# The second layer of a routed MLP with two blocks of 128 tokens per pass on the partitions, and w2 in row quarters

## Chip, core and metric

The kernel runs on one core of a Trainium2 chip. The metric is the device time of one execution in microseconds, the median of several runs. TensorE is called PE, VectorE DVE, ScalarE ACT, GpSimd POOL; SyncE (SP) only issues transfers here. Everything is fp32 unless said otherwise.

## What is computed

An RWKV-5 attention block is followed by a mixture-of-experts layer with one expert per token. The reference, cut:

```python
# attention: batch 4, 8 heads, 768 steps, head size 48
for t in range(S):
    cur = einsum('bhd,bhe->bhde', u * k_t, v_t)
    y[:, :, t] = einsum('bhd,bhde->bhe', r_t, state + cur)
    state = w * state + einsum('bhd,bhe->bhde', k_t, v_t)
# routing: N = 3072 tokens, 384 wide, 8 experts, hidden size 1024
logits = x @ w_gate
expert_idx = argmax(logits, axis=1)
gate_w = softmax(logits)[arange(N), expert_idx]
for e in range(E):
    mask = expert_idx == e
    h = maximum(x[mask] @ w1[e], 0)
    out[mask] = gate_w[mask] * (h @ w2[e])
```

## The kernel before

`straight` (line 42) does all the work, with the order of instructions on each engine written out by hand; `general` (line 672) is run instead only when a flag says that the data do not fit (an expert with more than 416 tokens, for one).

**Attention.** A loop of 16 steps (line 535), one for each batch and pair of heads, works in chunks of 128 time steps. In step i PE computes the own-token terms (`p_own`, line 263), the scores (275), the chunk states (298), the outputs of step i-1 (318, 323) and the transposition of step i-2 (`p_tr`, 336) so that tokens stand on partitions. ACT writes the diagonals (281) and copies the transposed outputs of step i-2 into the token buffer `xbs` of its batch (`keep`, 341 and 342; two buffers, so batch b+2 writes over batch b). POOL copies one element of `own` (542, so that it starts after DVE has read it), multiplies r and k for the next step (`pairs`, 250), and in most steps scales its keys (`keys`, 254). When the four steps of a batch are through, DVE picks each token's expert and a rank within the expert. POOL then sends each column of 128 tokens to the scratch tensor `rows` in HBM (`send`, 388), one row per token in the order of expert and rank, with the gate value and the token's number beside the token. The dictionary `sends` (503) says in which step of the loop which of the six columns of a batch go. In step 13 SP issues the loads of the early passes from `rows`; those of `rows` are ordered behind all sends put down before them.

**Experts.** Each expert has room for 416 tokens. For experts 0 and 1 the first 160 tokens are an early pass each, started while the last batch is still being routed; the late passes are the remaining 256 tokens of experts 0 and 1, and 416 tokens of each of experts 2 to 7. A pass does this:
- `load` (418): four transfers bring the tokens from `rows` into `xs`, 32 tokens by 32 columns at a time; there are three such buffers.
- `xT` (425): three DVE transposes of 32x32 blocks give the tokens with the features on the partitions.
- `L1` (430): for each of 8 hidden tiles of 128, three matmuls (line 435) with w1 as the stationary operand and all tokens of the pass moving; ACT applies the ReLU (437).
- `L2` (439): for each of 3 output tiles m, 8 matmuls (446) with a 128x128 block of w2 stationary and the tokens moving. A DVE transpose (448) turns the result back into 32x32 blocks. The three results stand in the PSUM banks `yps[0]`, `dsb`, `yps[1]` (`ybank`, line 68).
- `put` (477): DVE computes the destination of each piece and multiplies by the gate (488), and POOL scatters one group of 32 tokens after the other (491). A group is 128 pieces of 96 columns, so 416 tokens take 13 scatters.

Only the last pass (expert 7) has something else: its `L2` covers the first 160 tokens (`LAST`), and `tokens_out` (454) does the other 256 as two blocks of 128 tokens. There the tokens of the hidden layer are the stationary operand and w2 moves (467), in three pieces of 128 columns for each block; the token is then on the partition, the gate is a scalar per partition (470), and one scatter writes 128 whole rows (471). Gate and number for these come by a small load of their own (`load_ids`, 452). The two blocks use the banks `yps[0]` and `dsb`.

Each fp32 matmul of the program is two instructions in the profile; a hidden tile's w2 product of 416 tokens is thus two rows.

w1 of an expert is loaded in four quarters, w2 in three thirds, one for each m (`weights2`, 407); both have two buffers. All loads stand in one queue on SP, in the order of the program. The main loop (643) does for pass k: L1 of pass k; the transposes of pass k+1; w1 of expert e+2; then L2 and put of pass k-1 and the w2 of its expert plus 2; then the load of pass k+2. For the last pass L2 of pass 6 comes first, then L1 of pass 7, then the put of pass 6, L2 of pass 7 and `tokens_out`.

Of the kernel before, what the change touches and what calls it, by code (L numbers as in the profile page):

```python
# [17 lines left out]
B, H, S, D = 4, 8, 768, 48  # L18
E, F = 8, 1024
DM = H * D  # L20
N = B * S
HP = H // 2
# [19 lines left out]
def straight(tc, rk, vk, w, w1, w2, out, flag):  # L42
# [20 lines left out]
    dsb = pp.tile([128, 512], FP32, name="dsb")  # L63
    tr = pp.tile([128, 512], FP32, name="tr")
# [3 lines left out]
    ybank = [yps[:, 0, :], dsb, yps[:, 1, :]]  # L68
# [95 lines left out]
    pos2 = cp.tile([128, 4], FP32, name="pos2")  # L164
    it = cp.tile([128, 64], I32, name="it")
# [39 lines left out]


    w1s = [[cp.tile([128, DT, FQ], FP32, name=f"w1s{i}{q}") for q in range(4)] for i in range(2)]
    w2s = [[cp.tile([128, FT, 128], FP32, name=f"w2s{i}{m}") for m in range(DT)] for i in range(2)]
    ge = EARLY // 32

    def buffers(pool, n, k, x=None):
# [5 lines left out]
    early_bufs = [buffers(cp, EARLY, f"e{k}") for k in range(2)]  # L217
    cnt = cp.tile([128, E], FP32, name="cnt")
# [185 lines left out]
        for q in range(4):  # L404
            nc.sync.dma_start(w1s[e % 2][q], w1[e % E, q])

    def weights2(e, ms=range(DT)):
        for m in ms:
            nc.sync.dma_start(w2s[e % 2][m], w2[e % E, m])

    class Pass:
        def __init__(self, e, s0, n, bufs=None):
            self.e, self.s0, self.n = e, s0, n
            self.g = n // 32
            if bufs:
                self.x, self.t, self.h, self.y, self.yo, self.ix = bufs

        def load(self):
            for a in range(4):
                nc.sync.dma_start(  # L420
                    self.x[32 * a:32 * a + 32, 0:self.g, :],
                    rows[self.e * N + self.s0:self.e * N + self.s0 + self.n, a * Q:(a + 1) * Q].rearrange(
                        "(g j) c -> j g c", j=32))

        def xT(self):
            for m in range(DT):
# [9 lines left out]
                                     rhs=self.t[:, m, 0:self.n], start=m == 0, stop=m == DT - 1, skip_group_check=True)  # L436
                nc.scalar.activation(h[:, f, 0:self.n], p[:, 0:self.n], func=ACT.Relu)  # L437

        def L2(self, ms=range(DT), n=None):
            n = n or self.n  # L440
            g = n // 32
            y = self.y
            for m in ms:
                p = ybank[m]
                for f in range(FT):
                    nc.tensor.matmul(p[:, 0:n], lhsT=w2s[self.e % 2][m][:, f, :],  # L446
                                     rhs=self.h[:, f, 0:n], start=f == 0, stop=f == FT - 1, skip_group_check=True)
                nc.vector.transpose(y[:, 0:g, 32 * m:32 * m + 32], p[:, 0:n].rearrange("p (g j) -> p g j", j=32))  # L448

        def load_ids(self):  # L450

            nc.sync.dma_start(xg, rows[self.e * N + LAST:self.e * N + CAP, 2 * D:2 * D + 2].rearrange("(t p) c -> p t c", p=128))

        def tokens_out(self):

            nc.vector.tensor_scalar(out=vt, in0=pos2[:, 0:nl], scalar1=float(LAST), scalar2=cnt[:, self.e:self.e + 1],
                                    op0=ALU.add, op1=ALU.is_lt)
            nc.vector.memset(it2, 1 << 20)
            nc.vector.tensor_scalar(out=ia, in0=xg[:, :, 1].bitcast(I32), scalar1=2, scalar2=None,
                                    op0=ALU.logical_shift_right)  # L460
            nc.vector.copy_predicated(it2, vt, ia)
            for t in range(nl):
                p, y = ybank[t], yt[t].rearrange("p (a m i) -> p m a i", a=HP, m=DT)
                for m in range(DT):
                    o = p[:, m * 128:(m + 1) * 128]
                    for f in range(FT):
                        nc.tensor.matmul(o, lhsT=self.h[:, f, LAST + t * 128:LAST + (t + 1) * 128],  # L467
                                         rhs=w2s[self.e % 2][m][:, f, :], start=f == 0, stop=f == FT - 1,
                                         skip_group_check=True)
                nc.vector.tensor_scalar_mul(y, p[:, 0:DM].rearrange("p (m a i) -> p m a i", a=HP, m=DT), xg[:, t, 0:1])  # L470
                s_ = nc.gpsimd.indirect_dma_start(
                    out=out[:, :], out_offset=bass.IndirectOffsetOnAxis(ap=it2[:, t:t + 1], axis=0),
                    in_=yt[t][:, :], in_offset=None, bounds_check=N - 1, oob_is_err=False)
                tc.declare_no_dep(s_.ins, group="sc", reason="each token stands in one row")
                tc.add_to_no_dep_group("sc", s_.ins)

        def put(self, n=None):

            yo, ix, g = self.yo, self.ix, (n or self.n) // 32
            ids = self.x[:, 0:g, 2 * D + 1].bitcast(I32)  # L480
            if self.s0 == 0 and self.n == EARLY:
                nc.vector.tensor_copy(ix[:, 0:g], ids)
            else:
                nc.vector.tensor_scalar(out=vm[:, 0:g], in0=pos[:, 0:g], scalar1=float(self.s0), scalar2=cnt[:, self.e:self.e + 1],
                                        op0=ALU.add, op1=ALU.is_lt)
                nc.vector.memset(ix[:, 0:g], 1 << 20)
                nc.vector.copy_predicated(ix[:, 0:g], vm[:, 0:g], ids)
            nc.vector.tensor_tensor(yo[:, 0:g, :], self.y[:, 0:g, :], bc(self.x[:, 0:g, 2 * D:2 * D + 1], [128, g, 2 * D]),  # L488
                                    op=ALU.mult)
            for k in range(g):  # L490
                s_ = nc.gpsimd.indirect_dma_start(  # L491
                    out=out4[:, :], out_offset=bass.IndirectOffsetOnAxis(ap=ix[:, k:k + 1], axis=0),
                    in_=yo[:, k, :], in_offset=None, bounds_check=N * HP - 1, oob_is_err=False)
                tc.declare_no_dep(s_.ins, group="sc", reason="each token stands in one row")
                tc.add_to_no_dep_group("sc", s_.ins)

    LAST = 160
    early = [Pass(e, 0, EARLY, early_bufs[e]) for e in range(2)]
    late = [Pass(e, EARLY, CAP - EARLY) for e in range(2)] + [Pass(e, 0, CAP) for e in range(2, E)]

    sends = {}
    for b in range(B - 1):
        for k, cs in enumerate(((0,), (1, 2), (3, 4, 5)) if b < B - 2 else ((0,), (1, 2, 3, 4, 5))):
            sends[4 * b + 6 + k] = (b, cs)

    selection()
# [26 lines left out]
    for i in range(1, U):  # L535
        b, k = divmod(i - 6, 4)
# [78 lines left out]
    mp = P.enter_context(tc.tile_pool(name="mp", bufs=1))  # L615
    bufs = [buffers(mp, CAP, k) for k in range(2)]
    xss = [bufs[0][0], bufs[1][0], mp.tile([128, ng, Q], FP32, name="xs2")]
    for k, p in enumerate(late):
        _, p.t, p.h, p.y, p.yo, p.ix = bufs[k % 2]
        p.x = xss[k % 3]  # L620
    vm = mp.tile([128, ng], I32, name="vm")
    nl = (CAP - LAST) // 128
    xg = mp.tile([128, nl, 2], FP32, name="xg")
    vt, it2, ia = [mp.tile([128, nl], I32, name=n) for n in ("vt", "it2", "ia")]
    yt = [mp.tile([128, DM], FP32, name=f"yt{k}") for k in range(nl)]

    in_range()
    count(cnt)
# [7 lines left out]
    late[-1].load_ids()  # L636
    for p in early:
        p.L2()
        p.put()
# [24 lines left out]


# [6 lines left out]
def general(tc, rk, vk, w, w1, w2, out):  # L672
# [270 lines left out]
                half(b, hp, hf, kT, rT, vt, St, xb)  # L943
        gate(b, xb)
    for e in range(E):
        for m in range(DT):
            nc.scalar.dma_start(w2_all[:, e, :].rearrange("p (f m j) -> p m f j", m=DT, j=128)[:, m], w2[e, m])
    att.close()


# [181 lines left out]
def _layout(inputs):  # L1132
# [23 lines left out]
    w2 = x["moe_w2"].reshape(E, FT, 128, HP, DT, 32).transpose(0, 2, 1, 4, 3, 5).reshape(E, 128, FT, DT, 128)  # L1156
    w2 = w2.transpose(0, 3, 1, 2, 4)
# [20 lines left out]
```

## Time and profile before

| | us |
|---|---|
| median of 3 runs | 404.15 (403.97 to 406.21) |
| the profiled execution | 427.2 |
| its span, first to last instruction | 425.5 |
| PE busy | 397.4 |
| POOL busy | 187.0 |
| DVE busy | 137.8 |
| ACT busy | 122.5 |
| matmuls of L1, late passes (435) | 126.0 |
| matmuls of L2, late passes (446) | 76.7 into yps, 38.3 into dsb |
| scatters of the late passes (491), 86 | 83.6 |
| sends to rows (388), 24 | 26.0 |

All times but the first row are from one profiled execution. Busy time of PE counts each matmul from start to its modelled end, so neighbours overlap; the distance between starts is what a matmul costs in a stream. A view by lines groups the instructions of one line; the chain of work follows the last instruction back to what released it; the timeline lists instructions in order of time, with the idle time before each and what ended it in brackets. "issue" and "remote" mean that the trace shows no releaser.

### The profile page before, as it was taken

How to read it: one execution, taken by the hardware profiler on the slowest of the kernel's cores; microseconds unless marked ns; L12 is line 12 of the kernel's file. 1: busy time of each engine (PE TensorE's matmuls, PEld its weight loads, DVE VectorE, ACT ScalarE, POOL GpSimd, SP SyncE). 2: the span in 40 equal slices, each digit the busy share in tenths (PEclk: the TensorE clock that was granted, in tenths of full speed). 3: DMA queues.
4: the chain of work that ended last, by engine and by line, in shares of the span. 5: the costliest groups of instructions: out<-in, count | busy, mean ns of one | idle time of the engine just before them, and what ended most of it. 6: DMA issues, size and time to landing. Idle time of an engine off the chain costs nothing.

```text
span 425.5 us, 7326 instructions
## 1 busy us (share of the span) xinstructions
PE 397.4 (93%) x2869; PEld 284.1 (67%) x2869; DVE 137.8 (32%) x284; ACT 122.5 (29%) x348; POOL 187.0 (44%) x194
## 2 busy tenths in 40 slices
PE   7999997998989997999999999999999999996992
PEld 6788876787868996887585555555555554553692
DVE  8975876875731123011103012112112102120020
ACT  2786866776543301210201101101100200000100
POOL 2587778688450436002506104703702720767041
PEclk9999999997879999999999999999999999997998
DMA  8995978488790251766547336335435633112201
GB/s 213 272 270 145 321 219 252 141 256 289 204 390 27 81 132 50 191 179 182 155 136 195 97 99 170 109 114 148 151 95 146 176 99 100 42 45 95 80 21 45
DMA packets 33739, 65.22 MB, mean 153 GB/s; under 512 B 17975, under 2 KB 19011, under 8 KB 33696
## 3 DMA queue, kind: packets, MB, share of 16 engines
q1 hardware_dynamic: 28960, 54.83, 44.7%
q0 software_dynamic: 4736, 9.84, 6.6%
q8 instruction: 24, 0.39, 0.4%
q14 instruction: 19, 0.16, 0.1%
HBM read 53.55 MB, written 11.50 MB: 153 GB/s over the span
## 4 chain that ended last, share of the span: by engine, by line
PE 88%; DVE 3%; issue 3%; DMA 2%; another core or an unknown queue 1%; POOL 1%; ACT 0%; SPq 0%; POOLq 0%; DVEq 0%
PE X L435 33%; PE yps L446 20%; PE dsb L446 10%; PE X L275 6%; PE yps L318 6%; PE tr L336 4%; PE yps L323 3%; DMA rk<-in_rk_dram 2%; PE dsb L298 2%; PE dsb L263 1%; PE X L336 1%; PE yps L467 1%; PE dsb L467 1%; DVE RK L244 1%
## 5 line engine op out<-in xcount | busy, mean ns | idle before, releaser
L491 POOL DMA_INDIRECT out_dram<-yo,ix x86 | 83.6, 972 | 159.6 <-DVE yo L488 92.6
L435 PE MATMUL X<-xT,w1s 128*128 128x416 f32 (+1 forms) x384 | 126.0, 488 | 7.2 <-issue 6.2
L435 PEld LDWEIGHTS X<-xT,w1s 128*128 128x128 f32 x384 | 74.0, 194 | 57.5 <-issue 52.7
L437 ACT ACTIVATE hT<-X 128x416 f32<-128x416 f32 (+1 forms) x64 | 30.8, 484 | 220.9 <-PE X L435 176.8
L446 PE MATMUL yps<-hT,w2s 128*128 128x416 f32 (+2 forms) x256 | 76.7, 453 | 0.7 <-DVE yq L448 0.7
L446 PEld LDWEIGHTS yps<-hT,w2s 128*128 128x128 f32 x256 | 47.0, 190 | 28.8 <-issue 25.8
L281 ACT ACTIVATE A<-ident,own 128x128 f32<-128x128 f32 x192 | 57.9, 388 | 7.4 <-DVE own L267 5.3
L448 DVE STREAM_TRANSPOSE yq<-yps 128x416 f32<-128x416 f32 (+2 forms) x16 | 8.7, 541 | 126.1 <-PE yps L446 121.1
L446 PE MATMUL dsb<-hT,w2s 128*128 128x416 f32 (+2 forms) x128 | 38.3, 452 | 0.0
L275 PE MATMUL X<-RK 48*128 48x128 f32 x384 | 31.9, 294 | 2.0 <-DVE RK L244 1.4
L446 PEld LDWEIGHTS dsb<-hT,w2s 128*128 128x128 f32 x128 | 23.5, 190 | 13.6 <-issue 12.7
L388 POOL DMA_INDIRECT rows<-xb,slot x24 | 26.0, 1082 | 14.8 <-issue 8.4
L275 PEld LDWEIGHTS X<-RK 48*128 48x128 f32 x384 | 24.8, 189 | 9.1 <-issue 5.7
L318 PE MATMUL yps<-A,vk 128*48 128x128 f32 x384 | 27.6, 292 | 1.3 <-issue 1.3
L244 DVE TENSOR_TENSOR RK<-rk,TT 112x1536 f32<-112x1536 f32 x16 | 27.6, 1728 | 0.2
L542 POOL COPY turn<-own 1x1 f32<-1x1 f32 x14 | 20.0, 1426 | 17.2 <-DVE own L267 16.7
L250 POOL TENSOR_TENSOR rp<-rk 112x768 f32<-112x768 f32 x15 | 27.3, 1818 | 0.0
L427 DVE STREAM_TRANSPOSE xT<-xs 128x416 f32<-128x416 f32 (+1 forms) x24 | 11.7, 540 | 47.9 <-DMA xs<-rows 41.5
L318 PEld LDWEIGHTS yps<-A,vk 128*48 128x48 f32 x384 | 22.6, 131 | 4.6 <-issue 2.9
L287 DVE COPY_PREDICATED A<-strict,X 128x512 f32<-128x512 int32 x32 | 22.9, 733 | 4.4 <-ACT A L281 2.5
L328 ACT COPY yT<-yps 112x384 f32<-112x384 f32 x32 | 13.7, 480 | 17.9 <-PE yps L323 12.2
L336 PE MATMUL tr<-sel,yT 112*128 112x104 f32 x128 | 18.9, 293 | 0.0
(121 smaller groups left out, 321.3 us busy)
## 6 DMA issues: line engine op xcount, KB each, us to landing
w1s<-in_w_dram SPq DMA_DIRECT2D x40, 384.0 KB
w2s<-in_w_dram SPq DMA_DIRECT2D x24, 512.0 KB
rk<-in_rk_dram SPq DMA_DIRECT2D x16, 672.0 KB
vk<-in_vk_dram SPq DMA_DIRECT2D x16, 528.0 KB
xs<-rows SPq DMA_DIRECT2D x24, 169.0 KB
out_dram<-yo,ix POOLq DMA_INDIRECT x86
rows<-zt SPq DMA_DIRECT2D x1, 1248.0 KB
xs<-rows SPq DMA_DIRECT2D x8, 104.0 KB
```

Of the source, the lines that this page charges most:

```text
L244: nc.vector.tensor_tensor(RKs[i % 3][0:KP].rearrange("p u (c t) -> p u c t", t=C), x[0:KP].rearrange("p u (c t) -> p u c t", t=C), bc(TT[: ...
L250: (eng or nc.gpsimd).tensor_tensor(rps[i % 2][0:KP], x[0:KP, 0], x[0:KP, 1], op=ALU.mult)
L275: nc.tensor.matmul(o, lhsT=r[q, 1, c * C:(c + 1) * C], rhs=r[q, 0, c * C:(c + 1) * C], start=True, stop=True, skip_group_check=True)
L281: nc.scalar.activation(A[:, place(c, h), :], ident, func=ACT.Copy, scale=own[i % 2][:, c, h:h + 1])
L287: nc.vector.copy_predicated(A[:, 4 * k:4 * k + 4, :], bc(m[:, None, :], [128, 4, C]), X01[k])
L318: nc.tensor.matmul(o(c, h), lhsT=v[:, c, h * D:(h + 1) * D], rhs=A[:, place(c, h), :], start=c < 2, stop=c == 0, skip_group_check=True)
L336: nc.tensor.matmul(trv[c // 4][:, c % 4, :], lhsT=yTs[i % 3][0:KP, c & 1, (c // 2) * C:(c // 2 + 1) * C], rhs=sel[:, c & 1, i % HP, :], st ...
L388: s_ = nc.gpsimd.indirect_dma_start(out=rows[:, :], out_offset=bass.IndirectOffsetOnAxis(ap=slot[b % 2][:, c:c + 1], axis=0), in_=xbs[b % ...
L435: nc.tensor.matmul(p[:, 0:self.n], lhsT=w1s[self.e % 2][f // 2][:, m, f % 2 * 128:(f % 2 + 1) * 128], rhs=self.t[:, m, 0:self.n], start=m ...
L437: nc.scalar.activation(h[:, f, 0:self.n], p[:, 0:self.n], func=ACT.Relu)
L446: nc.tensor.matmul(p[:, 0:n], lhsT=w2s[self.e % 2][m][:, f, :], rhs=self.h[:, f, 0:n], start=f == 0, stop=f == FT - 1, skip_group_check=True)
L491: s_ = nc.gpsimd.indirect_dma_start(out=out4[:, :], out_offset=bass.IndirectOffsetOnAxis(ap=ix[:, k:k + 1], axis=0), in_=yo[:, k, :], in_o ...
```

## The change

In every late pass, the last 256 tokens now go through `tokens_out`, and `L2` with `put` covers only what is left: nothing for experts 0 and 1, 160 tokens for experts 2 to 7. `tokens_out` multiplies by w2 in one piece of 384 columns per hidden tile instead of three of 128. For all passes but the last it goes through the hidden tiles with both blocks side by side; for the last it finishes one block before the other. The blocks use the banks `tr` and `dsb`. w2 is cut into four quarters of two hidden tiles, all 384 columns each, in HBM and in the buffers. Each late pass has the small load of gates and numbers behind its token load (three buffers); the destinations and results of the blocks have two buffers. In the loop over steps, the sends of batches 0 and 1 go as columns 0, then 1 and 2, then 3 and 4, then 5, in four successive steps, where they went as 0, then 1 and 2, then 3 to 5 in three. In the last iteration the put of pass 6 comes ahead of L1 of pass 7.

```diff
-    w2s = [[cp.tile([128, FT, 128], FP32, name=f"w2s{i}{m}") for m in range(DT)] for i in range(2)]
+    w2s = [[cp.tile([128, 2, DM], FP32, name=f"w2s{i}{q}") for q in range(4)] for i in range(2)]
...
-    def weights2(e, ms=range(DT)):
-        for m in ms:
-            nc.sync.dma_start(w2s[e % 2][m], w2[e % E, m])
+    def weights2(e):
+        for q in range(4):
+            nc.sync.dma_start(w2s[e % 2][q], w2[e % E, q])
...
         def load(self):
+            r = self.e * N + self.s0
             for a in range(4):
...
+            if self.nt:
+                nc.sync.dma_start(self.xg, rows[r + self.nf:r + self.n, 2 * D:2 * D + 2].rearrange("(t p) c -> p t c", p=128))
...
-        def L2(self, ms=range(DT), n=None):
+        def L2(self):
+            n, g = self.nf, self.nf // 32
+            if not n:
+                return
             y = self.y
-            for m in ms:
+            for m in range(DT):
                 p = ybank[m]
                 for f in range(FT):
-                    nc.tensor.matmul(p[:, 0:n], lhsT=w2s[self.e % 2][m][:, f, :],
+                    nc.tensor.matmul(p[:, 0:n], lhsT=w2s[self.e % 2][f // 2][:, f % 2, m * 128:(m + 1) * 128],
                                      rhs=self.h[:, f, 0:n], start=f == 0, stop=f == FT - 1, skip_group_check=True)
...
+            self.put()
...
+        def tokens_out(self, together=True):
...
+            def product(t, f):
+                c = self.nf + t * 128
+                nc.tensor.matmul(tbank[t][:, 0:DM], lhsT=self.h[:, f, c:c + 128], rhs=w2s[self.e % 2][f // 2][:, f % 2, :],
+                                 start=f == 0, stop=f == FT - 1, skip_group_check=True)
+            if together:
+                for f in range(FT):
+                    for t in range(nt):
+                        product(t, f)
+            for t in range(nt):
+                if not together:
+                    for f in range(FT):
+                        product(t, f)
+                nc.vector.tensor_scalar_mul(self.yt[t].rearrange("p (a m i) -> p m a i", a=HP, m=DT),
+                                            tbank[t][:, 0:DM].rearrange("p (m a i) -> p m a i", a=HP, m=DT),
+                                            self.xg[:, t, 0:1])
+                scatter(out, it2[:, t:t + 1], self.yt[t][:, :], N)
...
+    tbank = [tr, dsb]
-    late = [Pass(e, EARLY, CAP - EARLY) for e in range(2)] + [Pass(e, 0, CAP) for e in range(2, E)]
+    late = [Pass(e, EARLY, CAP - EARLY, 2) for e in range(2)] + [Pass(e, 0, CAP, 2) for e in range(2, E)]
...
-        for k, cs in enumerate(((0,), (1, 2), (3, 4, 5)) if b < B - 2 else ((0,), (1, 2, 3, 4, 5))):
+        for k, cs in enumerate(((0,), (1, 2), (3, 4), (5,)) if b < B - 2 else ((0,), (1, 2, 3, 4, 5))):
             sends[4 * b + 6 + k] = (b, cs)
...
             if k > 0:
                 o.L2()
-                o.put()
+                o.tokens_out()
                 weights2(o.e + 2)
         else:
             o.L2()
+            o.tokens_out()
             p.L1()
             weights1(p.e + 2)
-            o.put()
         if k + 2 < n:
             late[k + 2].load()
-    p.L2(n=LAST)
-    p.put(LAST)
-    p.tokens_out()
+    p.L2()
+    p.tokens_out(together=False)
```

More of the change, by code (lines that the diff above doesn't have):

```diff
@@ L405, in weights1, with __init__ @@
             nc.sync.dma_start(w1s[e % 2][q], w1[e % E, q])
-    def weights2(e, ms=range(DT)):
-        for m in ms:
-            nc.sync.dma_start(w2s[e % 2][m], w2[e % E, m])
+    def weights2(e):
+        for q in range(4):
+            nc.sync.dma_start(w2s[e % 2][q], w2[e % E, q])
     class Pass:
-        def __init__(self, e, s0, n, bufs=None):
-            self.e, self.s0, self.n = e, s0, n
+        def __init__(self, e, s0, n, nt, bufs=None):
+            self.e, self.s0, self.n, self.nt = e, s0, n, nt
+            self.nf = n - 128 * nt
             self.g = n // 32
@@ L418, in load @@
         def load(self):
+            r = self.e * N + self.s0
             for a in range(4):
[L420 to L423, printed above, removed]
+                nc.sync.dma_start(self.x[32 * a:32 * a + 32, 0:self.g, :],
+                                  rows[r:r + self.n, a * Q:(a + 1) * Q].rearrange("(g j) c -> j g c", j=32))
+            if self.nt:
+                nc.sync.dma_start(self.xg, rows[r + self.nf:r + self.n, 2 * D:2 * D + 2].rearrange("(t p) c -> p t c", p=128))
         def xT(self):
@@ L437, in L1 @@
                 nc.scalar.activation(h[:, f, 0:self.n], p[:, 0:self.n], func=ACT.Relu)
-        def L2(self, ms=range(DT), n=None):
-            n = n or self.n
-            g = n // 32
+        def L2(self):
+            n, g = self.nf, self.nf // 32
+            if not n:
+                return
             y = self.y
-            for m in ms:
+            for m in range(DT):
                 p = ybank[m]
                 for f in range(FT):
-                    nc.tensor.matmul(p[:, 0:n], lhsT=w2s[self.e % 2][m][:, f, :],
+                    nc.tensor.matmul(p[:, 0:n], lhsT=w2s[self.e % 2][f // 2][:, f % 2, m * 128:(m + 1) * 128],
@@ L447, in L2 @@
                                      rhs=self.h[:, f, 0:n], start=f == 0, stop=f == FT - 1, skip_group_check=True)
                 nc.vector.transpose(y[:, 0:g, 32 * m:32 * m + 32], p[:, 0:n].rearrange("p (g j) -> p g j", j=32))
[L450 to L475, printed above, removed]
@@ L477, in put @@
-        def put(self, n=None):
-            yo, ix, g = self.yo, self.ix, (n or self.n) // 32
+            self.put()
+        def put(self):
+            yo, ix, g = self.yo, self.ix, self.nf // 32
             ids = self.x[:, 0:g, 2 * D + 1].bitcast(I32)
@@ L490, in put @@
             for k in range(g):
[L491 to L498, printed above, removed]
@@ L499, in straight @@
-    late = [Pass(e, EARLY, CAP - EARLY) for e in range(2)] + [Pass(e, 0, CAP) for e in range(2, E)]
+                scatter(out4, ix[:, k:k + 1], yo[:, k, :], N * HP)
+        def tokens_out(self, together=True):
+            nt, it2 = self.nt, self.it2
+            nc.vector.tensor_scalar(out=vt, in0=pos2[:, 0:nt], scalar1=float(self.s0 + self.nf),
+                                    scalar2=cnt[:, self.e:self.e + 1], op0=ALU.add, op1=ALU.is_lt)
+            nc.vector.memset(it2, 1 << 20)
+            nc.vector.tensor_scalar(out=ia, in0=self.xg[:, :, 1].bitcast(I32), scalar1=2, scalar2=None,
+                                    op0=ALU.logical_shift_right)
+            nc.vector.copy_predicated(it2, vt, ia)
+            def product(t, f):
[14 more added lines that the diff above has]
+                scatter(out, it2[:, t:t + 1], self.yt[t][:, :], N)
@@ new lines, in scatter @@
+    def scatter(to, at, x, n):
+        s_ = nc.gpsimd.indirect_dma_start(out=to[:, :], out_offset=bass.IndirectOffsetOnAxis(ap=at, axis=0),
+                                          in_=x, in_offset=None, bounds_check=n - 1, oob_is_err=False)
+        tc.declare_no_dep(s_.ins, group="sc", reason="each token stands in one row")
+        tc.add_to_no_dep_group("sc", s_.ins)
+    tbank = [tr, dsb]
+    early = [Pass(e, 0, EARLY, 0, early_bufs[e]) for e in range(2)]
+    late = [Pass(e, EARLY, CAP - EARLY, 2) for e in range(2)] + [Pass(e, 0, CAP, 2) for e in range(2, E)]
@@ L617, in straight @@
     xss = [bufs[0][0], bufs[1][0], mp.tile([128, ng, Q], FP32, name="xs2")]
+    nt = 2
+    xgs = [mp.tile([128, nt, 2], FP32, name=f"xg{k}") for k in range(3)]
+    its = [mp.tile([128, nt], I32, name=f"it{k}") for k in range(2)]
+    yts = [[mp.tile([128, DM], FP32, name=f"yt{k}{t}") for t in range(nt)] for k in range(2)]
     for k, p in enumerate(late):
         _, p.t, p.h, p.y, p.yo, p.ix = bufs[k % 2]
-        p.x = xss[k % 3]
+        p.x, p.xg, p.it2, p.yt = xss[k % 3], xgs[k % 3], its[k % 2], yts[k % 2]
     vm = mp.tile([128, ng], I32, name="vm")
[L622 to L625, printed above, removed]
+    vt, ia = [mp.tile([128, nt], I32, name=n) for n in ("vt", "ia")]
     in_range()
@@ L635, in straight @@
     late[1].load()
-    late[-1].load_ids()
     for p in early:
         p.L2()
-        p.put()
     late[0].xT()
@@ L945, in general @@
     for e in range(E):
-        for m in range(DT):
-            nc.scalar.dma_start(w2_all[:, e, :].rearrange("p (f m j) -> p m f j", m=DT, j=128)[:, m], w2[e, m])
+        for q in range(4):
+            nc.scalar.dma_start(w2_all[:, e, 2 * q * DM:2 * (q + 1) * DM], w2[e, q].rearrange("p i c -> p (i c)"))
     att.close()
@@ L1155, in _layout @@
     w1 = w1.transpose(0, 3, 1, 2, 4)
-    w2 = x["moe_w2"].reshape(E, FT, 128, HP, DT, 32).transpose(0, 2, 1, 4, 3, 5).reshape(E, 128, FT, DT, 128)
-    w2 = w2.transpose(0, 3, 1, 2, 4)
+    w2 = x["moe_w2"].reshape(E, FT, 128, HP, DT, 32).transpose(0, 1, 2, 4, 3, 5).reshape(E, 4, 2, 128, DM)
+    w2 = w2.transpose(0, 1, 3, 2, 4)
     w = _np.concatenate([w, ub.reshape(KP, -1), wg.reshape(KP, -1)], axis=1)
```

## The prediction

> **What bounds the kernel now.** I read the page first (busy shares), then the chain of work that ended last, then the timeline around the token sends. The page:
>
> ```profile
> span 425.5 us, 7326 instructions
> PE 397.4 (93%) x2869; PEld 284.1 (67%) x2869; DVE 137.8 (32%) x284; ACT 122.5 (29%) x348; POOL 187.0 (44%) x194
> ```
>
> TensorE (PE) is busy nearly throughout; VectorE (DVE) and GpSimd (POOL), whose work the change cuts most, are under half busy. The chain in order of time (start, us, what), from its whole listing and from the same view of 340 us to the end:
>
> ```profile
> 213.26 3.45 PE yps L446 x16
> ...
> 346.53 5.59 PE dsb L446 x16
> 352.12 5.60 PE yps L446 x16
> 357.72 0.02 issue
> 357.74 0.63 DVE yq L448
> ...
> 385.92 3.36 issue
> 389.28 7.86 PE X L435 x12
> ...
> 402.26 2.17 PE dsb L446 x16
> 404.43 2.19 PE yps L446 x16
> 406.62 0.02 issue
> 406.64 0.36 DVE yq L448
> ...
> 407.05 5.62 PE yps L467 x48
> 412.67 5.37 PE dsb L467 x48
> ```
>
> From 165.19 us, when the first late pass starts, the chain is matmuls laid end to end: a pass costs what its matmuls stream. Only two DVE waits interrupt them: 357.72 to 358.41 (0.69 us: the second layer of pass 6 starts right after that of pass 5 and waits for the last transpose out of yps) and 406.62 to 407.05 (0.43 us: the token blocks reuse yps). One matmul instruction takes 2.17/16 = 135.6 ns for 160 columns, 3.45/16 = 215.6 for 256, 5.59/16 = 349.4 for 416, and 5.37/48 = 111.9 for 128.
>
> The third view is the timeline around the last sends of batch 1:
>
> ```profile
> 99.74 0.98 POOL L388 DMA_INDIRECT rows<-xb,slot  x1 [0.30 <-issue]
> 99.78 0.86 ACT L328 COPY yT<-yps 112x384 f32<-112x384 f32 x2 [1.86 <-remote]
> 99.82 0.17 DVE L400 TENSOR_TENSOR cnt<-dsb,basef 128x8 f32<-128x8 f32 x1 [2.27 <-remote]
> 100.13 0.51 PE L263 MATMUL dsb<-rp,wug 112*2 112x192 f32 x8 [1.96 <-DVE cnt L400]
> ```
>
> ACT and DVE both wait 2 us for nothing the trace names while POOL works through three sends. Are such stalls part of the 404.15? In the timeline L263 opens each step, and an undisturbed step takes 6.55 us (84.33 to 90.88). The steps from 61.07 to 129.04 exceed that by 0.86, 2.20, 0.55, 0, 2.70, 3.22, 0.18 and 5.86: 15.6 us. In the last pass the 3.36 us of "issue" is followed by 12 instructions at 655 instead of 349 ns (3.67 us more) and about 0.9 of small gaps: 7.9 us. Profiled time 427.2 (span 425.5 and 1.7 around it) less 23.5 leaves 403.7, against a median of 404.15. So I take these stalls as peculiar to the profiled execution: about 0.4 us of them can be in the median.
>
> **What the Trainium skill says.** "TensorE: Matmul & The Clock Gate", section "Back-to-back issue gap": a warm matmul of N columns takes N/2.4 + 2.5 ns. With two such streams and one floor per fp32 instruction that gives 135.8, 215.8 and 349.2, agreeing with 135.6, 215.6 and 349.4 above; at 128 it gives 109.2 and the trace has 111.9. The same page, "Part 1: The HAM clock gate": after an idle window of some 3.4 us the array runs at half clock; the 3.36 us gap and the 655 ns instructions agree, so a long PE wait costs nearly twice itself. "DMA: Bandwidth & Descriptors", section "Anatomy of one DMA — SWDGE (gpsimd) path": some 2.0 us fixed per DMA. The trace has 1.8 when the queues are quiet (last send ends 150.39, the load behind it issues 152.16) but 5.8 when they are loaded (100.72 to 106.53): there I use 5.8.
>
> **The change part by part.**
>
> Token blocks. A block of 128 tokens is 8 row tiles of two instructions each, 384 columns wide. No row shows 384; the slope from 160 to 416 columns, (349.4 - 135.6)/256 = 0.835 ns a column, gives 135.6 + 224 x 0.835 = 322.6 ns. Below it is bounded by the pure slope (320.6), above by 349.4. Two blocks: 32 x 322.6 = 10.32 us. Weight loads (190 ns in the groups) are shorter than that and stay hidden.
> - Passes 0 and 1 (256 late tokens): 3 x 3.45 = 10.35 becomes 10.32. Two: -0.06.
> - Passes 2 to 6 (416): 3 x 5.59 = 16.77 becomes 3 x 2.17 + 10.32 = 16.83. Five: +0.30.
> - Pass 7 already has 160 + 2 x 128, but with 96 instructions of 128 columns: 5.62 + 5.37 = 10.99 becomes 10.32: -0.67.
> The columns streamed are the same everywhere; only instruction count and width move. At the upper bound of 349.4 ns all eight passes together cost 8 x 32 x 27 ns = 6.9 us more; the steady slope makes that unlikely.
>
> Banks. Blocks go to tr and dsb. Pass 6's second layer then begins in yps, read last some 10 us earlier, so the 0.69 wait goes; its dsb part starts 2.17 us later, when the two copies (2 x 0.62 us, L470) that empty tr and dsb are done: 0.9 us of cover. Pass 7's first block no longer waits for yps: -0.43. The new wait inside each pass, the second block's dsb behind the transpose of m = 1, has 2.17 us of other matmuls plus a block-0 matmul against 0.35 us of transpose. That holds as long as DVE is free: its only blocking item is the next pass's xT, which runs 12 to 14 us earlier (231.88 against the first L448 at 246.01). Without that cover PE would wait for the load one for one.
>
> POOL and DVE. A pass of 13 scatters at 1.28 us (259.80 to 261.07) becomes 5 + 2, and 8 becomes 2: 42 fewer, 54 us of POOL time, all behind matmuls: worth 0 on the path. DVE's three 0.62 transposes and 1.45 multiply become three 0.35, 0.65, four small instructions (0.7) and two 0.62: the same total, also hidden. At the end the five scatters from 408.2 to 414.3 precede the block copies as now; the last copy, scatter and drain (418.07 to 425.5) are the same: 0.
>
> Loads. w2 goes from three to four transfers of the same total; each quarter is released as the f loop passes it, about when the thirds were, two passes before its use: 0. The second layer now needs all four quarters within its first 16 instructions, likewise long landed. The new xg load (256 pieces of 8 bytes, one issue of 0.45 us on SyncE's queue) sits behind a pass's four xs loads. It waits for the last token copy, 1.3 us after the pass's matmuls; behind it is the next w1 load, which waits some 4 us for the first layer anyway: 0.
>
> Sends. One send of batch 0 moves from step 8 to 9, one of batch 1 from 12 to 13. At step 13 POOL has turn 1.55, rp 1.81, Kd 1.19 from 101.84, so the send ends about 107.5 and lands (5.8) at 113.3; SyncE's early loads, issued at 106.53, wait for it, 6.8 us later, with w2 and w1 queued behind. Eight issues (4.38) and 2 us of landing: 119.7, against DVE's need at 126.90. Without the stalls the same sum, from the step's start, gives 17.4 us for the first early pass against a need at 19.0, and 19.6 against 19.7 for the second. It just fits: 0, with a loss of one for one beyond. keep in steps 10 and 14 waits some 2 us for the same landing; ACT has 1.2 us spare per step and PE uses keep's result a step later: 0, at most 0.7 each.
>
> Sum: -0.06 + 0.30 - 0.67 - 0.69 - 0.43 = -1.55 us. On the profiled execution 425.5 becomes 423.9 if its stalls recur; on the median 404.15 becomes 402.6.
>
> **Rivals.**
> 1. Late early loads, slower. Same send at step 13; if its landing takes over 7.4 us instead of 5.8, the first layer at the end of the loop waits one for one, plus the half clock. To end 1% slower it must outweigh -1.55 and add 4: a landing near 10 us if the clock drops too, 13 if not. For it: 5.8 is already thrice the quiet value, and DMA is 80 to 90% busy there. Against: the queue's backlog then is only one w1 load. About 409.
> 2. The profile's stalls are real and come from three sends in a row (2.20, then 2.70 and half clock 3.22); shorter bursts remove half: -4, 398.6. Against: only 0.4 us is left for them in the median.
> 3. A small new wait per pass (DVE late for dsb, or alternating banks costing 5% of 10.3 us a pass): 0.5 x 8 = +4 - 1.55, 406.6. Against: L275 alternates banks too and runs without gaps.
> 4. The POOL saving pays: it cannot, as no chain piece before the last scatter is POOL's in the late passes; it merges with the forecast.
>
> **How the numbers follow.** 1% is 4 us, about what a measurement of this kernel can tell from no change. Forecast at 402.6, its own range 401.3 to 404.2: 0.69. Rival 2: 0.11, all of it over 1% faster. Rival 3: 0.08, within 1%. Rival 1: 0.12, of which 0.09 over 1% slower and 0.03 within. So faster 0.11, same 0.80, slower 0.09. The range from 400.0 to 407.0 takes in rival 3 and the milder part of rival 1, and leaves out rival 2 and the rest of rival 1, 0.20 together.
>
> **What would show it.** In the profile after: L446 groups only at 160 columns; token matmuls near 322 ns apart, a middle pass 16.8 us of second layer; no DVE wait between passes 5, 6 and 7; 56 scatters; the xse load issued about 113 and still ahead of DVE. Wrong would be: gaps between token matmuls, a PE wait on DVE yq or on xse, or step times changed in the median itself.

## The result and the profile after

The changed kernel takes 401.70 us (median of 13 runs, 400.97 to 403.41) against 404.78 (13 runs, 403.76 to 406.21) for the kernel before: ratio 0.9933, 95% interval 0.9914 to 0.9952, or 2.7 us (1.9 to 3.5) less. The forecast was 402.6, 1.55 us less.

The page of the profile after; its execution took 401.49 us:

```profile
span 399.8 us, 7421 instructions
PE 386.1 (97%) x2933; PEld 284.9 (71%) x2933; DVE 136.1 (34%) x312; ACT 122.4 (31%) x348; POOL 146.8 (37%) x152
```

POOL has 40 us less to do, and PE is busy 97% of the span. The chain in order of time (start, us, what), pieces of one middle pass and of the last from its whole listing:

```profile
224.42 2.17 PE yps L454 x16
...
228.76 2.17 PE yps L454 x16
230.94 0.65 PE tr L487 x2
...
380.00 2.17 PE yps L454 x16
382.18 5.16 PE tr L487 x16
387.34 5.17 PE dsb L487 x16
```

Line 446 is now 454, line 467 is 487 and line 435 is 441. A block takes 16 instructions in 5.16 us, 322.5 ns each. The waits of 0.69 and 0.43 us are gone: 380.00 + 2.17 leads straight to 382.18. From 149.30 us to the last matmul at 392.51 PE has no idle time named in the waits at all, bar 1.6 us right at the start of pass 0. All steps of the attention loop are within 0.6 us of 6.55 from step 4 on.

The later sets of runs, each on a chip of its own, found the kernel before at 433 to 437 us, not 404, so each is compared only with the kernel before on its own chip. (Which chip the first runs had isn't known.) What differs is the subject of the experiments. Times in the table are medians of all runs, but the ratios leave out slow runs, those over 1.5% above the fastest of their kernel.

| kernel | us | before, same chip | ratio, 95% |
|---|---|---|---|
| changed, first runs | 401.70 | 404.78 | 0.9933 (0.9914 to 0.9952) |
| before, again | 437.04 | 437.13 | 1.0014 (0.9983 to 1.0045) |
| changed, old sends | 422.12 | 437.13 | 0.9654 (0.9601 to 0.9707) |
| before, new sends | 431.38 | 437.13 | 0.9865 (0.9800 to 0.9929) |
| changed, old bank | 421.65 | 437.13 | 0.9639 (0.9587 to 0.9690) |
| changed, again | 417.96 | 436.38 | 0.9644 (0.9532 to 0.9757) |
| changed, pieces of 128 columns | 422.42 | 436.38 | 0.9759 (0.9631 to 0.9887) |
| changed, later send | 419.69 | 436.38 | 0.9673 (0.9528 to 0.9819) |
| changed, scatters threefold | 516.12 | 436.38 | 1.1899 (1.1686 to 1.2111) |
| before, no scatters in pass 5 | 426.78 | 435.40 | 0.9793 (0.9722 to 0.9865) |
| changed, POOL busy | 414.37 | 435.40 | 0.9546 (0.9478 to 0.9614) |
| changed, early order | 413.43 | 435.40 | 0.9447 (0.9384 to 0.9510) |
| changed, early order, spaced sends | 408.03 | 432.85 | 0.9399 (0.9347 to 0.9452) |

### The profile page after: what moved, and what is told of

Same layout as the page of the kernel before. It is cut to its first block, busy times and chain, and to the rows that moved or that the text cites. A ratio compares the mean times of both kernels' runs of the same rounds, so it can differ in the third digit from the quotient of the medians.

```text
span 399.8 us, 7421 instructions
## 1 busy us (share of the span) xinstructions
PE 386.1 (97%) x2933; PEld 284.9 (71%) x2933; DVE 136.1 (34%) x312; ACT 122.4 (31%) x348; POOL 146.8 (37%) x152
## 4 chain that ended last, share of the span: by engine, by line
PE 93%; issue 3%; DVE 1%; POOL 1%; ACT 0%; POOLq 0%
PE X L441 34%; PE dsb L487 10%; PE tr L487 10%; PE yps L454 9%; PE X L275 7%; PE yps L318 6%; PE dsb L454 4%; PE tr L336 4%; PE yps L323 3%; PE dsb L298 2%; PE X L336 2%; PE dsb L263 2%; POOL rp L250 0%; DVE pw L124 0%; DVE yps L65 0%
## 5 line engine op out<-in xcount | busy, mean ns | idle before, releaser
L441 PEld LDWEIGHTS X<-xT,w1s 128*128 128x128 f32 x384 | 72.9, 190 | 49.7 <-issue 45.1
L504 POOL DMA_INDIRECT out_dram<-yo,ix x30 | 29.3, 978 | 124.3 <-DVE ia L481 117.0
L487 PE MATMUL tr<-w2s,hT 128*128 128x384 f32 x128 | 50.6, 486 | 0.0
L487 PE MATMUL dsb<-w2s,hT 128*128 128x384 f32 x128 | 50.6, 486 | 0.0
L504 POOL DMA_INDIRECT out_dram<-yt,it x16 | 15.7, 979 | 69.9 <-DVE yt L498 41.3
L487 PEld LDWEIGHTS dsb<-w2s,hT 128*128 128x128 f32 x128 | 24.3, 190 | 17.0
L388 POOL DMA_INDIRECT rows<-xb,slot x24 | 29.6, 1232 | 16.8 <-issue 6.4
L487 PEld LDWEIGHTS tr<-w2s,hT 128*128 128x128 f32 x128 | 24.0, 190 | 15.2 <-issue 0.3
L498 DVE TENSOR_SCALAR yt<-tr,xg 128x384 f32<-128x384 f32 x8 | 4.9, 617 | 71.3 <-PE tr L487 71.3
L454 PEld LDWEIGHTS yps<-hT,w2s 128*128 128x128 f32 x192 | 27.1, 190 | 1.9 <-issue 1.6
L454 PE MATMUL yps<-hT,w2s 128*128 128x160 f32 x192 | 28.0, 299 | 0.0
L456 DVE STREAM_TRANSPOSE yq<-yps 128x160 f32<-128x160 f32 x12 | 4.2, 350 | 68.2 <-PE yps L454 68.2
```

The source lines that it names most:

```text
L388: s_ = nc.gpsimd.indirect_dma_start(out=rows[:, :], out_offset=bass.IndirectOffsetOnAxis(ap=slot[b % 2][:, c:c + 1], axis=0), in_=xbs[b % ...
L441: nc.tensor.matmul(p[:, 0:self.n], lhsT=w1s[self.e % 2][f // 2][:, m, f % 2 * 128:(f % 2 + 1) * 128], rhs=self.t[:, m, 0:self.n], start=m ...
L454: nc.tensor.matmul(p[:, 0:n], lhsT=w2s[self.e % 2][f // 2][:, f % 2, m * 128:(m + 1) * 128], rhs=self.h[:, f, 0:n], start=f == 0, stop=f = ...
L487: nc.tensor.matmul(tbank[t][:, 0:DM], lhsT=self.h[:, f, c:c + 128], rhs=w2s[self.e % 2][f // 2][:, f % 2, :], start=f == 0, stop=f == FT - ...
L504: s_ = nc.gpsimd.indirect_dma_start(out=to[:, :], out_offset=bass.IndirectOffsetOnAxis(ap=at, axis=0), in_=x, in_offset=None, bounds_check ...
```

## The experiments

**The kernel before, a second time.** No edit. 

> The kernel before, unchanged, for a second profile. If the stalls of its first profile (15.6 us in the steps, 7.9 in the last pass) belong to that execution alone, this one's span is about 402 to 403 us, its steps are about 6.55 us throughout, and only the waits of 0.69 us (between passes 5 and 6) and 0.43 us (before the first token block) break the matmuls of the late passes. If they belong to the kernel, steps 8 and 9 and steps 12 and 13, with three token sends in a row, are again 1 to 3 us too long. The ratio is 1.000 by either theory.

Measured: 437.04 us, and the stalls are there again, in the same places (steps 8, 9, 12, 13 and 15 of the attention loop, and the last pass). So they don't belong to one profiled execution; the theory in the expectation that they do falls. The timeline of the last pass (start, us, engine, line, what, and in brackets the idle time before it):

```profile
384.18 0.52 ACT L437 ACTIVATE hT<-X 128x416 f32<-128x416 f32 x1 [36.52 <-issue]
389.07 20.41 SPq L405 DMA_DIRECT2D w1s<-in_w_dram  x4
389.13 0.52 ACT L437 ACTIVATE hT<-X 128x416 f32<-128x416 f32 x1 [4.44 <-remote]
389.71 6.15 PE L435 MATMUL X<-xT,w1s 128*128 128x416 f32 x12 [4.13 <-issue]
...
397.27 0.97 POOL L491 DMA_INDIRECT out_dram<-yo,ix  x1 [0.30 <-issue]
400.49 0.52 ACT L437 ACTIVATE hT<-X 128x416 f32<-128x416 f32 x1 [5.85 <-remote]
401.06 8.05 PE L435 MATMUL X<-xT,w1s 128*128 128x416 f32 x18 [5.21 <-ACT hT L437]
```

ACT, SP and PE stand still together and come back within 0.7 us of each other, while POOL puts out one scatter every 1.28 us, 26 for passes 5 and 6 with one pause of 1.45 us between the two passes, the last at 397.27. First-layer work that needs 16.8 us takes 29.8 (379.13 to 408.95). The size of this standstill isn't fixed: the same work takes 24.6 us in the first profile before (375.28 to 399.92) and 20.4 in the profile of the kernel before with new sends (376.17 to 396.56). It is no lack of DMA bandwidth: from 385 to 390 us the DMA engines are busy for 0.12 of the time, from 396 to 402 for 0.15. Nor does the trace have a transfer of instructions in these stretches; the next one starts at 411.57.

**Old sends in the changed kernel**, and **new sends in the kernel before.**

The cut shows the first edit; the second is the reverse.

```diff
-((0,), (1, 2), (3, 4), (5,)) if b < B - 2 else
+((0,), (1, 2), (3, 4, 5)) if b < B - 2 else
```

> The changed kernel with the token sends as before (columns 3 to 5 of a batch in one step). My theory: the sends bring nothing, all of the gain is in the late passes, so this stays at about 0.993 of before (401.7 us). Rival: the 1.2 us by which the gain exceeds my sum are the sends'; then this is about 403 us, 0.996. Third possibility, the moved send costs: then this is faster than the changed kernel.

> The kernel before with the new sends alone. My theory: 1.000 of before, within 0.3 us; the early load from rows goes out later by some 5 us in the profile, with nothing waiting for it. Rival, the sends brought the rest of the gain: 0.997, 1.2 us less. Rival, the late landing delays keep and the early load: over 1.000.

Measured: 0.9654 and 0.9865. The sizes expected were for a chip without stalls and don't apply. New sends alone gain, but the runs lie between 424.8 and 436.0. The profile (span 423.0, against 434.4 for the kernel before) splits its gain: step 9 takes 7.48 instead of 8.87 us, while most of the rest, 9.4 us, is the shorter standstill in the last pass, whose code is the same. The two kernels of this experiment also show that the sends are the smaller part: with the old sends the changed kernel is still 15 us ahead of the kernel before. What the sends are worth on the first chip no run shows.

**Old bank for the first block.**

```diff
-    tbank = [tr, dsb]
+    tbank = [yps[:, 0, :], dsb]
```

> The changed kernel with the first token block in the bank yps[0], as the last pass had it before, instead of tr. My theory, that the banks are worth 1.12 us in my sum: the waits come back, about 0.43 us ahead of the blocks in each of the six passes with 160 other tokens (2.6 us) and about 0.6 to 1.3 us where pass 6 follows pass 5 (its first matmuls need the bank that the last copy reads): 3 to 4 us in all, ratio 1.001 to 1.003 of before. If DVE is quick enough, or the wait follows the half of yps alone, it stays at 0.993.

Measured: 0.9639. The waits of PE from pass 0 on (us in total, times, longest):

```profile
PE X L441 <- issue: 2.9, 1, 2.9
PE yps L487 <- DVE yq L456: 2.7, 6, 0.4
```

The six waits came back at the size expected, 2.7 against 2.6 us; those between passes 5 and 6 did not, because the copy out of yps was done in time. Each wait costs more than its own length: in the chain the first pair of block matmuls behind it takes 0.91 us, where a pair otherwise takes 0.65. From the first layer of pass 3 to that of pass 7, which takes in five of these waits, PE needs 155.1 us (221.85 to 376.97), where the changed kernel needs 151.2 in its second profile (224.04 to 375.28); with the last pass it is 4.6 us in all, above the 3 to 4 expected. So moving one block to tr is worth 4.6 us beside blocks put into the old bank. The times are too scattered to show it: 0.9639 here and 0.9644 for the changed kernel on another chip. Beside the kernel before, only the wait of the last pass counts, 0.43.

**The changed kernel again.** No edit. 

> The changed kernel, unchanged, beside the kernel before on one chip, since the runs of the first four experiments stood at 437 us for the kernel before where the first runs stood at 404. If this chip is like the first: 0.992 to 0.995 of before. If it is like the second, where the kernel with old sends was at 0.965 and that with the old bank at 0.964: 0.95 to 0.96, and the profile has the stalls in steps 8 and 12 shorter than the kernel before, and none in the last pass.

Measured: 0.9644, near the second case, and the last pass is free of stalls: all 48 instructions of its first layer in one piece.

```profile
375.28 16.92 PE L441 MATMUL X<-xT,w1s 128*128 128x416 f32 x48
```

From the start of late pass 0 to PE's last matmul it needs 243.2 us (165.84 to 409.05) like the first profile after (149.30 to 392.51), where the kernel before needs 259.7 on its chip with stalls (167.35 to 427.06). That is 16.5 of the 18 us between the two spans. Of it 13.1 are the first layer of the last pass (29.8 us against 16.8), and 1.7 the first layer of passes 0 and 1, which runs partly at a lower clock in that profile of the kernel before (22.48 us against 20.80). Without these two the kernel before needs 245.0, and 1.8 us are left, beside the 1.55 that I had summed. The other 1.5 us of the 18 lie ahead of the late passes.

That the stalls in steps 8 and 12 would be shorter was wrong: 7.47 and 9.34 us, against 7.45 and 9.28 in the kernel before; only step 9 is (7.48 against 8.87). The attention steps of the changed kernel still lose time (step 13 at 98.94 takes 11.1 us here, step 15 12.6). In step 13 PE doesn't stand still but is slow: its granted clock is 0.50 from 101 to 107 us, behind a wait of 1.99. In the next experiment step 13 follows an equal wait (1.98), the clock stays at 1.00, and it takes 6.55.

**Pieces of 128 columns.** Each block's product becomes three of 128 columns, m outside f.

```diff
-tbank[t][:, 0:DM], ... rhs=w2s[self.e % 2][f // 2][:, f % 2, :]
+tbank[t][:, m * 128:(m + 1) * 128], ... rhs=w2s[self.e % 2][f // 2][:, f % 2, m * 128:(m + 1) * 128]
```

> The changed kernel with the token blocks in pieces of 128 columns (96 instructions instead of 32 for two blocks) in every late pass, as the last pass had them before. From 111.9 ns against the 322.5 ns now measured: 8 x (96 x 111.9 - 32 x 322.5) = 8 x 0.42 = 3.4 us more than the changed kernel. Rival, the weight loads hide and the pieces cost only their columns: 0.7 us more. Banks are no longer taken in turn, so if taking turns cost something this would be less than 3.4.

Measured: 422.42, 4.5 above the changed kernel, where 3.4 were expected and 0.7 by the rival. The intervals of the two ratios overlap, so the profile has to tell. The chain has these pieces for a block:

```profile
184.17 5.36 PE tr L487 x48
189.53 5.36 PE dsb L487 x48
```

5.36 against 5.16: 0.40 a pass, 3.2 in all; five passes lose 0.1 to 0.6 us in the second block besides, mostly in pauses that the trace gives no releaser for, so the late passes take 248.0 instead of 243.2 us. The width of the moving operand is worth at least what the durations say.

**A later send in step 13.**

```diff
+        if i == 13:
+            for _ in range(16):
+                nc.gpsimd.memset(zt, 0.0)
         if i in sends:
```

> The changed kernel with 16 writes of a scratch tile on POOL ahead of the send in step 13, which put it some 5.6 us later (0.35 us each). Rival 1 of the prediction, the late early load: in the profile of the changed kernel the eight loads were issued from 103.9 to 108.4, land some 3 us later, and DVE takes them at 113.3, so about 2 us are spare; then this is 3 to 4 us above the changed kernel, a wait of DVE on xse in the profile. If the spare time is larger than I see (the loads land within 2 us, or the two early passes are not both needed), 0 to 2 us.

Measured: 419.69, within the scatter of the changed kernel (414.4 to 420.4 for the latter). The timeline:

```profile
106.68 6.58 POOL L587 MEMSET zt<- 128x312 f32 x16
113.63 1.88 POOL L388 DMA_INDIRECT rows<-xb,slot  x1 [0.37 <-issue]
...
117.33 4.84 SPq L425 DMA_DIRECT2D xse<-rows  x8
...
124.07 1.46 DVE L433 STREAM_TRANSPOSE xTe<-xse 128x160 f32<-128x160 f32 x6
```

The send went out 7 us later and SP's loads with it, the last issued at 122.2, and DVE took them at 124.07 without a wait: they land within 1.9 us. My figure of 3 us to landing was too long, and the late early load (rival 1) falls: 7 us of delay cause no wait. In the first profile after, the cover is larger still (loads issued by 108.4, taken at 113.29).

**Every scatter three times.** For all but the last pass, two more scatters of the same data go to scratch tensors.

```diff
+        for to_ in [to] + [(j if n == N else j4) for j, j4 in (junk if e < E - 1 else [])]:
             s_ = nc.gpsimd.indirect_dma_start(out=to_[:, :], ...
```

> The changed kernel with each scatter of the passes 0 to 6 and the early ones put out three times, the second and third into scratch tensors (work added; the output is the same). POOL has 21 scatters a pass instead of 7, more than the 13 of the kernel before. My theory that POOL's scatters are hidden: 0 to 0.5 us above the changed kernel. Rival, long runs of scatters stall the other engines, and that was part of the gain: 3 us or more, with waits of PE and ACT for nothing named during the scatters.

Measured: 516.12, 98 us above the changed kernel. My theory that scatters are hidden falls. The timeline from the scatters of the early passes (157.28 to 195.48) into late pass 0:

```profile
175.26 0.98 POOL L507 DMA_INDIRECT junk<-yoe,ixe  x1 [0.31 <-issue]
176.25 0.38 ACT L445 ACTIVATE hT<-X 128x256 f32<-128x256 f32 x1 [26.36 <-DMA junk<-yoe,ixe]
...
187.84 12.31 SPq L407 DMA_DIRECT2D w1s<-in_w_dram  x2
187.84 0.38 ACT L445 ACTIVATE hT<-X 128x256 f32<-128x256 f32 x1 [11.21 <-remote]
188.08 0.98 POOL L507 DMA_INDIRECT out_dram<-yoe,ixe  x1 [0.31 <-issue]
188.28 4.66 PE L443 MATMUL X<-xT,w1s 128*128 128x256 f32 x12 [14.36 <-issue]
...
199.04 0.38 ACT L445 ACTIVATE hT<-X 128x256 f32<-128x256 f32 x1 [10.82 <-remote]
```

ACT has its input and runs only at 176.25, 187.84 and 199.04. At 187.84 SP and PE come back with it; PE has its next piece only behind ACT's of 199.04. POOL alone keeps going, with a scatter every 1.28 us. In the waits from late pass 0 on, PE loses 43.8 us to ACT's hT and 22.6 to nothing named. The tripled traffic isn't what holds them: from 176 to 188 us the DMA engines are busy for 0.10 to 0.12 of the time.

**The kernel before without the scatters of pass 5.** The rows of expert 5 are left out of the output.

```diff
-            for k in range(g):
+            for k in range(0 if self.e == 5 else g):
```

> The kernel before without the 13 scatters of pass 5 (expert 5); those rows of the output are left out. In the kernel before, the scatters of passes 5 and 6 follow each other without a pause, 26 in 33 us, and on the chip of its second profile PE and ACT stand still in the last pass while they run (4.1 and 5.2 us, and half clock after). Theory, a run of scatters stalls the other engines once it is long enough: on a chip with stalls the last pass loses them, 9 to 13 us less than before; on a chip without, as the first, 1.000. Rival, the stalls belong to the last pass for another reason (its loads of w1, its order): unchanged on either chip.

Measured: 426.78, ratio 0.9793, 8.6 to 9 us less, just under what was expected. The timeline of the last pass:

```profile
382.77 16.92 PE L435 MATMUL X<-xT,w1s 128*128 128x416 f32 x48
399.53 2.06 PE L446 MATMUL yps<-hT,w2s 128*128 128x160 f32 x14
```

48 instructions in one piece, so in this profile the whole standstill of the last pass is gone. Part of that is lost elsewhere: step 9 takes 13.0 us instead of 8.87, with a granted clock of 0.50 from 74 to 83 us. The loads, the order and the 13 scatters of pass 6 are as before; only the run of scatters is cut from 26 to 13. So its length makes the standstill, and the rival falls. This also settles it for the change itself, which moved the put of pass 6 as well: without any move, the shorter run is enough.

**POOL busy, but not with scatters.**

```diff
         tc.add_to_no_dep_group("sc", s_.ins)
+        for _ in range(2 if e < E - 1 else 0):
+            nc.gpsimd.memset(idle, 0.0)
```

> The changed kernel with two writes of a scratch tile of 1150 columns (about 1.3 us each) on POOL behind each scatter, where the kernel with threefold scatters had two more scatters (516 us). If the stalls there come from POOL being busy without a pause, this is as slow, over 500 us on a chip with stalls. If they come from the scatters themselves (their transfers or the making of them), this stays within 1 us of the changed kernel.

Measured: 414.37, ratio 0.9546, no slower than the changed kernel, which stood at 0.9644 on another chip; closer than their intervals the two can't be compared. POOL in pass 2:

```profile
243.67 0.98 POOL L504 DMA_INDIRECT out_dram<-yo,ix  x1 [18.06 <-DVE ia L481]
244.63 2.20 POOL L509 MEMSET idle<- 128x1150 f32 x2
246.99 0.97 POOL L504 DMA_INDIRECT out_dram<-yo,ix  x1 [0.16 <-issue]
```

POOL works 23 us on end, and from late pass 0 on PE waits 1.6 us in all. POOL without a pause is harmless as such; long runs of scatters close behind each other are not.

**Two early waits taken away.** The second early pass has the banks tr, dsb, yps[1], and late pass 0's transposes stand ahead of its last one on DVE.

```diff
-    for p in early:
-        p.L2()
-    late[0].xT()
+    early[0].L2()
+    early[1].L2([tr, ybank[1], ybank[2]], late[0].xT)
```

> The changed kernel with two waits taken away that both kernels have around the early passes: the second early pass has the bank tr for its first third (its wait for the last transpose out of yps is 0.44 us), and the three transposes of late pass 0 stand ahead of the last transpose of the second early pass on DVE (PE waits 1.57 us for them now, 2.9 on the second chip). If the tokens of pass 0 have landed by then (issued from 137.6 to 139.4 in the profile of the changed kernel, some 5 us to landing, needed at 145.9): 1.5 to 2.0 us less than the changed kernel. If they land later: 0.4 us less.

Measured: 413.43, ratio 0.9447; on the same chip the changed kernel with harmless POOL work was at 0.9546. From the first early matmul to late pass 0 it needs 32.6 us (129.26 to 161.83) against 34.9 in the first profile after (114.43 to 149.30): 2.3 less, both waits gone, where 1.5 to 2.0 were expected.

**Spaced sends.** On top of that, four scratch writes between the five sends of step 15.

> The kernel with the early waits taken away (0.945 of before on its chip), and with four writes of a scratch tile (1.6 us) between the five sends that follow each other in step 15. On the chips with stalls that step lasts 12.5 instead of 6.55 us in every profile. Theory, taken from the threefold scatters and from the scratch writes behind them: a pause between scatters keeps the other engines from standing still; then step 15 lasts 7 to 8 us, and the ratio is 0.93 to 0.935. Rival, the stalls of the attention steps come with the transfers of the sends while the queues are full, whatever their spacing: step 15 stays above 11 us, ratio about 0.945. On a chip without stalls both give 0.988 to 0.989.

Measured: 408.03, ratio 0.9399. The timeline of step 15, from the longest of the six runs (409.82 us):

```profile
120.25 0.98 POOL L390 DMA_INDIRECT rows<-xb,slot  x1 [0.16 <-issue]
121.22 1.63 POOL L389 MEMSET zt<- 128x312 f32 x4
123.23 0.98 POOL L390 DMA_INDIRECT rows<-xb,slot  x1 [0.37 <-issue]
...
124.90 1.90 PE L443 MATMUL X<-xTe,w1s 128*128 128x160 f32 x12
```

Step 15 lasts from 118.35 to 124.90, 6.55 us, where it took 12.5 in the kernel without the pauses (116.73 to 129.26). There PE stood still between the sends:

```profile
123.05 0.89 PE L318 MATMUL yps<-A,vk 128*48 128x128 f32 x4 [0.74 <-issue]
124.51 0.88 PE L318 MATMUL yps<-A,vk 128*48 128x128 f32 x4 [0.57 <-issue]
125.93 1.95 PE L318 MATMUL yps<-A,vk 128*48 128x128 f32 x15 [0.55 <-issue]
...
129.26 2.04 PE L441 MATMUL X<-xTe,w1s 128*128 128x160 f32 x12
```

That step 15 takes 12.5 us in every profile, as I had written, isn't so: it takes 6.55 with the later send in step 13, 7.89 with pieces of 128 columns, 10.07 with the old bank and 10.23 with POOL busy. In these the sends come later and the standstill falls behind the step: from the start of step 15 to late pass 0 they need 48.1 to 49.2 us, like the changed kernel's second profile (49.1). With the early waits taken away it is 45.1, and with the pauses 39.1. So the pauses bring 6.0 us and don't only move the loss. The rival of full queues falls too: from 117 to 129 us the DMA share is as high with the pauses as without (0.93 to 1.04 and 0.97 to 1.04). Pauses of 2 us cure the standstill of that step; steps 8 to 13, where the sends were left, still have their losses. The ratio is short of the 0.93 to 0.935 that I expected of it, and two chips can't be compared to that precision.

## Why the prediction was right, and where it was wrong

- **Blocks of 384 columns.** 322.6 ns forecast, 322.5 measured; a middle pass has 6.51 + 10.32 us of second layer as summed. Right. Pieces of 128 columns confirm the counterpart of the sum. One reading was loose: the section "Back-to-back issue gap" of "TensorE: Matmul & The Clock Gate" in the Trainium skill gives N/2.4 + 2.5 ns for an isolated matmul, with other figures for a stream of weight loads and matmuls. That the streams here follow it, with 322.5 ns for two times 384 columns, is what this trace shows.
- **The two waits.** Gone, as forecast, and nothing took their place: no PE wait on yq in the profile after. They were slightly undersized: the 16 instructions behind the first wait took 5.85 us (358.41) and not the 5.59 of the sum, so 0.26 more goes with it. Putting the old bank back brings 0.44 us of wait for each pass, and 0.26 for the pair behind it.
- **keep waits some 2 us for a landing.** The profile after has this wait, and no loss behind it. The timeline of ACT in step 10:

```profile
81.88 0.33 ACT L342 COPY xb<-X 128x208 f32<-128x208 f32 x1 [2.16 <-DMA rows<-xb,slot]
```

- **The clock.** The prediction took an idle window of some 3.4 us ahead of half clock from the Trainium skill ("TensorE: Matmul & The Clock Gate", "Part 1: The HAM clock gate"). In these traces a shorter wait can be enough: the clock is at 0.50 from 104 to 107 us in the profile before, in the step that opens behind a wait of 1.96, and in step 13 of the changed kernel's second profile behind 1.99. It needn't come, as the 1.98 above show.
- **Loads and quarters of w2.** 0 forecast, and no PE or DVE wait for w2s or xg in the profile after.
- **The early load.** I put its issue at about 113 from a profile with stalls; it is issued at 103.89, 2.4 us after the send's end and not 5.8, and 7 us of delay cost nothing. The step was too careful, the zero was right.
- **The size.** -1.55 forecast, -2.7 (-1.9 to -3.5) measured. In the late passes the profiles agree with the sum: 252.85 us before (165.19 to 418.04), less the 7.9 of standstill, against 243.21 after, 1.8 us less, and the 0.26 above is the difference. So about 1 us (0.2 to 1.7) lies elsewhere.
- **The stalls.** The step that failed is their reading: "I take these stalls as peculiar to the profiled execution", with "42 fewer, 54 us of POOL time ... worth 0 on the path" and rival 4, "it cannot". They recur in all later sets of runs of the kernel before. The arithmetic that 23.5 us less leaves the median was true of the first chip only, and it described a chip without standstill, not a kernel without it. On the other chips, shorter runs of scatters (7 a pass instead of 13, and at most 6 without a pause in passes 5 to 7, where 26 followed each other) bring 13 of the 18 us; threefold scatters and the missing ones of pass 5 show that from both sides. Rival 2 was right that the stalls are real, and wrong on where the gain lies: the new sends shorten step 9 by 1.4 us, and most of the rest is the late scatters.
- **Luck.** The mechanism of the 1.55 us held. That the total held too is owed to the chip of the first runs: on the one chip where both kernels ran unchanged in the later sets, the ratio was 0.9644, some 15 us less, and the forecast would have had a tenth of the gain.
- **Still open.** Whether the 1 us on the first chip is a small remainder of the same standstill, or the sends, no run settles: there is no profile of the kernel before from such a chip. The prediction's 403.7 for a run without stalls is 1.1 below the median of the 13 runs, 404.78, which would fit a remainder. And what the waiting engines lack while POOL scatters, and why the chips differ so much in it, is open too. The trace names no releaser. That it goes with the length of the run in the last pass, and with the pauses between the sends in step 15, is shown; the mechanism isn't. Length alone doesn't describe it: in the attention steps two or three sends in a row are enough for waits of 2 us.

## What to carry to other kernels

Price a run of indirect transfers by its length and not only by POOL's time: cut it by making each scatter write whole rows, or, as shown for the five sends of step 15, put 2 us of other POOL work between two of them. When a profile is 5% above the timed runs, its stalls are a warning of what another chip may do; look at which engine alone keeps running in them before setting them aside. Where PE is the bound, widening the moving operand and giving back-to-back products banks of their own are gains that the durations of one profile give closely (1.55 us summed, 1.8 found in the late passes); count with each wait that the first matmuls behind it take longer, 0.26 us here.

## What was not expected of the hardware

- In long runs of scatters, PE, ACT and SP stand still together and come back within 0.7 us of each other (389.07 to 389.71 in the second profile of the kernel before); in the threefold kernel ACT ran only at 176.25, 187.84 and 199.04, 11.6 and 11.2 us apart. The DMA engines were busy for 0.08 to 0.15 of the time meanwhile. A run of 13 (16.6 us) showed no standstill of PE in passes 2 to 4; one of 26, with a single pause of 1.45 us in its middle, cost 3.6, 7.9 and 13.1 us in three profiles. Between the five sends of step 15, 1.6 us of other POOL work took the standstill away.
- The same kernel, without an edit, took 404.8 us in the first set of runs and 433 to 437 on the four chips of the later sets. The profile taken for the prediction (427.2 us) has the stalls too and lies outside the 13 runs of the first set (403.76 to 406.21).
